# Long convolution by FFT, then a phase layer: group 0 takes h's spectrum from setup's tiles, and the e table is made during the first inverse

## Chip, cores and metric

One core of one Trainium2 chip. The metric is the device time of one execution in microseconds (us), the median of several runs. All inputs and outputs lie in the chip's memory in float32.

## What is computed

The input x has 8 batches of 5696 positions by 128 channels; h has 5696 positions by 128 channels. The reference, cut to what matters:

```python
L = 2 * S                                   # S = 5696
Yf = rfft(x, n=L, axis=1) * rfft(h, n=L, axis=0)[None]
x = irfft(Yf, n=L, axis=1)[:, :S, :]        # a causal convolution, channel by channel
theta = x @ w_theta
zr, zi = x * cos(theta), x * sin(theta)
y = einsum('ts,bsd->btd', w_tok_r, zr) + einsum('ts,bsd->btd', w_tok_i, zi)
u = x + y
out = u + maximum(u @ w_ch, 0)
```

The change touches only the convolution's front: the tables, the transform of h, and the first of eight groups.

## The kernel before

**Stages.** The transform of length 11392 is done as 178 by 64, by matrix products on TensorE (PE). The work is cut into eight groups: two batches (`bp`) times 64 of the 128 channels (`dh`). For each group: stage a (PE line L241: x times the table `f1_t`, sixteen chunks, evicted to the tile `a_` by ACT at L248 or by DVE at L246); stage b (L259, with the table `w_t2`, twelve chunks of eight frequencies: ACT copies a chunk to `xs` at L372, DVE multiplies it at L374 with the chunk `hs` of h's spectrum into the tiles `u_t` and `v_t`); stage c (L390 and L391, with the tables `r_u` and `r_v`, sixteen chunks, evicted to `g` by DVE at L398 or by ACT at L395 and L396, the latter ones alternately); stage d (L413, with the table `e_t`, evicted to `yt` by ACT at L416, and stored). Stage c needs every chunk of stage b. Beside stage c of one group runs stage a of the next, beside stage d its stage b. The loop over the groups is unrolled; `woven` lays several lists of steps into one order by their shares of an interval. All stages rotate four PSUM buffers of two banks.

**h.** h goes through stages a and b first (`h16`, then `h_chunk`, L297 and L299). `h_chunk` writes its twelve chunks into `u_t` and `v_t`, which the groups' products need later, and stores each with two DMAs into `hf_hbm` (L304). Every group then loads its half of a chunk from `hf_hbm` with two DMAs into one of four `hs` buffers (L365): four chunks ahead, and the chunk c+4 when chunk c has been multiplied. All these DMAs are issued by SP, in order.

**Tables.** `w_t2` comes in three blocks of fifteen frequencies: `w_angles(b)` takes four DVE operations (the third of them `below_one`, L164, and the rounding before it `up`, L161), `w_sines(b)` two on ACT, and `w_rest(b)` four copies or negations on DVE (L204 to L207). `e_t` (33 rows) comes in three steps of eleven rows: `e_index` on POOL (an index, a scaling, the rounding), `e_angles` on DVE, `e_table` as two sines on ACT (L170, L173); all three steps are woven into group 0's stage b. They use the pool `s2`.

**x.** `load_x` loads x for two batches by 16 DMAs that POOL issues (L133). There is one buffer `x16`, so the load for the next pair of batches waits until PE has read the old one, which is at the end of the odd group's stage a.

**Order.** Up to the end of group 0's stage a (`in_order`), DVE, ACT and POOL run in the order of the source. After that a scheduler orders each engine's instructions by priority. Within an engine everything starts in order, and an instruction that waits holds up all behind it. POOL executes its arithmetic and issues its DMAs from one queue.

Of the kernel before, what the change touches and what calls it, by code (L numbers as in the profile page):

```python
# [23 lines left out]
def kernel(  # L24
# [80 lines left out]
    def pool(name, bufs, stack, **kw):  # L105
        return stack.enter_context(tc.tile_pool(name=name, bufs=bufs, **kw))
# [5 lines left out]
    keep = pool("keep", 1, ctx, side="right")  # L112
    fc = pool("fft_c", 1, conv, side="right")
    fs = pool("fft_s", 2, conv, side="right")
    s1 = pool("set_1", 1, setup, side="right")
    s2 = pool("set_2", 3, setup, side="right")

    u_t = fc.tile([P, UVW + P], F16)
    v_t = fc.tile([P, UVW + P], F16)
# [31 lines left out]
    def pair_of(n, m=P):
        t = s2.tile([P, 11 * NB], F32, tag="turn", name="turn")[:m, :n]
        k = s2.tile([P, 11 * NB], F32, tag="whole", name="whole")[:m, :n]
        return t, k
# [5 lines left out]
    def up(t, k, eng=nc.vector):  # L160
        eng.tensor_scalar(k, t, MAGIC, None, op0=add)  # L161
# [15 lines left out]
    f1_t = fc.tile([P, 2 * K1], F16)  # L177
    odd = lane[:, 4:5]
    WS = 15
    w_of = [pair_of(WS * 32) for _ in range(KH // WS)]  # L180
    f_t, f_k = (z[:NB, :K1] for z in (s1.tile([P, K1], F32, name="f_t"), s1.tile([P, K1], F32, name="f_k")))
    o_t, o_k = s1.tile([P, 1], F32, name="o_t"), s1.tile([P, 1], F32, name="o_k")

    def slot(e, k1):
        return (k1 + e * KH) % K1

    def w_angles(b):
        t, k = w_of[b]
        nc.vector.tensor_scalar(t, k, lane[:, 2:3], lane[:, 3:4], op0=add, op1=mult)
        up(t, k)  # L190
        below_one(t, k)
        absolute(k, t)

# [13 lines left out]
            nc.vector.tensor_copy(w_t2[p0:p0 + 64, KH + s0:KH + s0 + WS],  # L207
                                  w_t2[64 - p0:P - p0, s0:s0 + WS])

    index(w_of[0][1], [[1, WS], [N1, 32]], 0)  # L210
    nc.vector.tensor_scalar(lane[:, 3:4], lane[:, 0:1], 1.0 / NF, None, op0=mult)
    w_angles(0)
    w_sines(0)
    index(f_k, [[1, K1]], 0)
    nc.vector.tensor_scalar(f_t, f_k, lane[:NB, 1:2], 1.0 / N1, op0=mult, op1=mult)
    up(f_t, f_k)
    below_one(f_t, f_k)
    absolute(f_k, f_t)
    sine(f1_t[:NB, K1:], f_t, -1)
    cosine(f1_t[:NB, :K1], f_k)  # L220
    for b in range(1, len(w_of)):
        index(w_of[b][1], [[1, WS], [N1, 32]], WS * b)
        w_angles(b)
        w_sines(b)
# [64 lines left out]
    nc.gpsimd.memset(hst[(NCK - 1) // 6][:, (NCK - 1) % 6], 0.0)  # L289

    def h_chunk(c):
        c0, ck = CHK[c]
        ps = f2(a_h, c, False)
        h_ = hst[c // 6][:, c % 6]
        dst = h_[:, :, :, :ck]
        if c % 3 == 1:
            nc.vector.tensor_scalar(dst, ps, 16.0 / NF, None, op0=mult)  # L297
        else:
            nc.scalar.activation(dst, ps, AF.Copy, scale=16.0 / NF)  # L299
        for cc, j in ((0, 0), (NCK - 1, CHK[-1][1] - 1)):  # L300
            if c == cc:
                nc.vector.tensor_scalar(dst[:, :, :, j], dst[:, :, :, j], 0.5, None, op0=mult)
        for ri in range(2):
            nc.sync.dma_start(  # L304
                hf_hbm[:, c, :, ri, :].rearrange("h p n -> p h n"),
                h_[64 * ri:64 * ri + 64].rearrange("p h d k -> p h (d k)"))

    for c in range(NCK):
        h_chunk(c)
    nc.gpsimd.memset(u_t[:, UVW:], 0.0)  # L310
    nc.gpsimd.memset(v_t[:, UVW:], 0.0)
# [4 lines left out]
    sgn = fc.tile([P, N2], F32)  # L316

    def r_table(n_, r_):
        t, k = pair_of(2 * N2)
# [12 lines left out]
    e_of = {}  # L332

    def e_index(n0):
        e_of[n0] = t, k = pair_of(11 * NB, K1)
        index(k, [[1, 11], [N2, NB]], n0)
# [8 lines left out]
    def e_table(n0):
        t3, k3 = (z.rearrange("p (n m) -> p n m", m=NB) for z in e_of[n0])
        sine(e_t[:K1, n0:n0 + 11, 1, :], t3, -1)
        cosine(e_t[:K1, n0:n0 + 11, 0, :], k3)
# [4 lines left out]

    LEAD = 4

    def stage_b(a_st, dh):

        hs_of = {}

        def load(c):  # L360
            if c >= NCK:
                return
            hs = hs_of[c] = fh.tile([P, 2, HD * CK], F16, tag="hs", name="hs")
            for e in range(2):
                nc.sync.dma_start(hs[64 * e:64 * e + 64], hf_hbm[dh, c])  # L365

        def chunk(c):
            c0, ck = CHK[c]
            hv = hs_of[c].rearrange("p r (d k) -> p r d k", k=CK)
            ps = f2(a_st, c)  # L370
            xs = fs.tile([P, 2, HD, CK], F16, tag="xs", name="xs")
            nc.scalar.activation(xs[:, :, :, :ck], ps, AF.Copy)  # L372
            for r in range(2):
                nc.vector.tensor_tensor(  # L374
                    uv[r][:, :, :, c0:c0 + ck], xs[:, :, :, :ck],
                    hv[:, r:r + 1, :, :ck].to_broadcast([P, 2, HD, ck]), op=mult)
            load(c + LEAD)
        return [lambda c=c: load(c) for c in range(LEAD)], [lambda c=c: chunk(c) for c in range(NCK)]
# [73 lines left out]

# [777 lines left out]
```

## Time and profile before

| | us |
|---|---|
| median of 3 runs (2083.46 to 2084.41) | 2083.66 |
| profiled execution | 2080.49 |
| its span, first to last instruction | 2078.7 |
| first PE instruction | 19.4 |
| h's stage b on PE, from | 34.1 |
| group 0: last product of stage b ends | 79.8 |
| group 0: stage c from, stage d from | 79.5, 100.9 |
| group 1: stage c from | 125.5 |

In the whole span PE is busy for 1960.0 us (94%), DVE for 1572.9 (76%), POOL for 921.9 (44%), ACT for 651.4 (31%). The granted clock of PE averages 0.983.

How to read it: the profile is of one execution. A line of the timeline has the start, the duration, the engine, the line of the kernel, the operation, the tiles written and read, the shape, how many instructions are merged in it, and in brackets how long the engine stood idle before it and what ended that. `SPq` and `POOLq` are instructions that only issue a DMA. Engines: PE is TensorE (PEld its weight loads), DVE is VectorE, ACT is ScalarE, POOL is GpSimd, SP is SyncE. The granted clock is the share of TensorE's full clock.

### The profile page before, as it was taken

How to read it: one execution, taken by the hardware profiler on the slowest of the kernel's cores; microseconds unless marked ns; L12 is line 12 of the kernel's file. 1: busy time of each engine (PE TensorE's matmuls, PEld its weight loads, DVE VectorE, ACT ScalarE, POOL GpSimd, SP SyncE). 2: the span in 40 equal slices, each digit the busy share in tenths (PEclk: the TensorE clock that was granted, in tenths of full speed). 3: DMA queues.
4: the chain of work that ended last, by engine and by line, in shares of the span. 5: the costliest groups of instructions: out<-in, count | busy, mean ns of one | idle time of the engine just before them, and what ended most of it. 6: DMA issues, size and time to landing. Idle time of an engine off the chain costs nothing.

```text
span 2078.7 us, 41648 instructions
## 1 busy us (share of the span) xinstructions
PE 1960.0 (94%) x15853; PEld 1079.2 (52%) x15853; DVE 1572.9 (76%) x2874; ACT 651.4 (31%) x989; POOL 921.9 (44%) x1663
## 2 busy tenths in 40 slices
PE   4688988889999999999999999899999999999998
PEld 4677888754444444444444444344444444444444
DVE  8666767777788888888877666877868677777767
ACT  5677878873333333333310000011111111111111
POOL 7302011257445454545466654445453535445450
PEclk9899999999999999999999999999999999999999
DMA  9879595989899999999999899778696978878793
GB/s 128 140 127 176 137 144 175 245 260 238 144 179 167 183 168 170 169 182 169 181 164 161 127 210 256 125 124 154 126 156 127 153 130 148 145 138 150 129 156 88
DMA packets 454312, 334.98 MB, mean 161 GB/s; under 512 B 134823, under 2 KB 407335, under 8 KB 453127
## 3 DMA queue, kind: packets, MB, share of 16 engines
q0 software_dynamic: 272032, 156.73, 57.2%
q1 hardware_dynamic: 176096, 164.05, 27.5%
q10 hardware_dynamic: 5984, 11.54, 1.6%
q8 instruction: 124, 2.03, 0.4%
q14 instruction: 76, 0.62, 0.1%
HBM read 377.11 MB, written 92.49 MB: 226 GB/s over the span
## 4 chain that ended last, share of the span: by engine, by line
PE 68%; DMA 3%; DVE 3%; POOL 2%; issue 2%; ACT 0%; DVEq 0%; ACTq 0%; SPq 0%; POOLq 0%
PE m L1167 61%; PE m L1088 2%; DMA b<-z_hbm 1%; DMA ring<-in_moe_w_tok_r_dram 1%; DVE c L1174 1%; DVE b L723 1%; PE v L869 1%; PE utp L862 1%; PE m L1171 1%; POOL ring L577 1%; POOL b L513 1%; DVE wt L782 1%; PE theta_ps L464 0%; PE tpz L810 0%; POOL y_hbm L651 0%
## 5 line engine op out<-in xcount | busy, mean ns | idle before, releaser
L577 POOL DMA_DIRECT2D ring<-in_moe_w_tok_i_dram x720 | 388.7, 546 | 655.6 <-DVE wt L782 571.7
L577 POOL DMA_DIRECT2D ring<-in_moe_w_tok_r_dram x720 | 387.2, 545 | 141.8 <-DVE wt L782 77.8
L782 DVE STREAM_TRANSPOSE wt<-ring 128x384 f32<-128x384 f32 (+2 forms) x720 | 359.3, 523 | 117.3 <-PE m L1167 68.2
L1167 PE MATMUL m<-b,wt 128*128 128x512 bf16 x1640 | 389.7, 380 | 2.0 <-DVE wt L782 1.7
L1167 PEld LDWEIGHTS <-wt 128*128 128x128 bf16 x1804 | 176.4, 98 | 219.8 <-DVE wt L782 7.8
L1174 DVE TENSOR_TENSOR c<-c,m 128x512 f32<-128x512 f32 x412 | 265.0, 668 | 0.4 <-PE m L1167 0.4
L864 ACT ACTIVATE ring<-utp 128x512 bf16<-128x512 bf16 x85 | 50.8, 597 | 581.9 <-PE utp L862 581.9
L390 PE MATMUL ps<-r_u,u_t 128*128 128x128 f16 x1024 | 122.4, 220 | 9.0 <-ACT red L487 3.7
L133 POOL DMA_DIRECT2D x<-in_x_dram x64 | 51.8, 818 | 166.4 <-PE ps L241 152.5
L391 PE MATMUL ps<-r_v,v_t 128*128 128x128 f16 x1024 | 121.4, 220 | 0.4
L1088 PE MATMUL m<-b,wt 128*128 128x512 bf16 x480 | 113.7, 387 | 7.5 <-DMA b<-z_hbm 4.4
L859 ACT ACTIVATE ub<-c 128x512 bf16<-128x512 f32 x88 | 55.1, 628 | 191.8 <-DMA ring<-in_moe_w_tok_r_dram 113.1
L391 PEld LDWEIGHTS <-v_t 128*128 128x128 f16 x1024 | 100.3, 98 | 9.6 <-issue 8.0
L390 PEld LDWEIGHTS <-u_t 128*128 128x128 f16 x1024 | 100.5, 98 | 4.2 <-DVE u_t L374 2.4
L374 DVE TENSOR_TENSOR u_t<-xs,hs 128x1024 f16<-128x1024 f16 x96 | 64.2, 668 | 50.4 <-DMA hs<-hf_hbm 25.6
L372 ACT ACTIVATE xs<-ps 128x1024 f16<-128x1024 f32 x96 | 91.4, 977 | 27.1 <-DVE v_t L374 12.3
L1088 PEld LDWEIGHTS <-wt 128*128 128x128 bf16 x528 | 51.5, 100 | 68.8 <-issue 11.0
L259 PEld LDWEIGHTS <-w_t 64*128 64x128 f16 x3240 | 60.7, 102 | 37.9 <-issue 31.6
L466 ACT ACTIVATE red<-theta_ps,magic 128x512 f32<-128x512 f32 (+1 forms) x46 | 31.6, 687 | 134.4 <-PE theta_ps L464 106.4
L812 ACT ACTIVATE ring<-tpz 128x512 bf16<-128x512 bf16 (+1 forms) x46 | 27.5, 597 | 131.1 <-PE tpz L810 110.6
L374 DVE TENSOR_TENSOR v_t<-xs,hs 128x1024 f16<-128x1024 f16 x96 | 63.6, 662 | 4.0 <-DMA hf_hbm<-v_t 4.0
L488 ACT ACTIVATE mag<-mag,half_pi 128x512 f32<-128x512 f32 (+1 forms) x90 | 65.6, 729 | 0.0
(2913 smaller groups left out, 3803.9 us busy)
## 6 DMA issues: line engine op xcount, KB each, us to landing
ring<-in_moe_w_tok_r_dram POOLq DMA_DIRECT2D x352, 96.0 KB, 4.5
ring<-in_moe_w_tok_i_dram POOLq DMA_DIRECT2D x352, 96.0 KB, 4.9
ring<-in_moe_w_tok_r_dram POOLq DMA_DIRECT2D x352, 80.0 KB, 4.4
ring<-in_moe_w_tok_i_dram POOLq DMA_DIRECT2D x352, 80.0 KB, 3.8
hs<-hf_hbm SPq DMA_DIRECT2D x192, 128.0 KB, 3.2
cp_hbm<-c SPq DMA_DIRECT2D x88, 256.0 KB, 2.4
c<-cp_hbm SPq DMA_DIRECT2D x88, 256.0 KB, 4.3
out_dram<-c SPq DMA_DIRECT2D x88, 256.0 KB, 4.1
```

Source lines behind the costliest of these rows:

```text
L259: nc.tensor.matmul(ps[:, e, j * HD:(j + 1) * HD], w_t2[rows, slot(e, c0 + j), N2 * (1 - ri):N2 * (3 - ri)], a_st["a"][rows, ri * K1 + c0 + ...
L372: nc.scalar.activation(xs[:, :, :, :ck], ps, AF.Copy)
L374: nc.vector.tensor_tensor(uv[r][:, :, :, c0:c0 + ck], xs[:, :, :, :ck], hv[:, r:r + 1, :, :ck].to_broadcast([P, 2, HD, ck]), op=mult)
L390: nc.tensor.matmul(o, u_t[:, at:at + P], r_u, start=True, stop=False)
L391: nc.tensor.matmul(o, v_t[:, at:at + P], r_v, start=False, stop=True)
L488: nc.scalar.activation(mag, mag, AF.Sin, bias=half_pi[:m], scale=-TWO_PI)
L577: nc.gpsimd.dma_start(wb[32 * i:32 * i + 32, :ng, :nj * 64], bass.AP(tensor=a.tensor, offset=a.offset + row0 * S + p * H + i * QR + j0 * 6 ...
L782: nc.vector.transpose(wt.rearrange("p j t r -> p (j t r)").bitcast(F32).rearrange("p (j g t) -> p g j t", j=TJ, g=4)[:, :ng, :nj], wb[:, : ...
L859: nc.scalar.activation(ub[:m].rearrange("p b d -> p (b d)"), c[:m], AF.Copy)
L1088: nc.tensor.matmul(ms[n // 2 * 2 + h], a[n][:, j, :, r], bts_of[p][jj][n % 2 * 2 + h][:, r, :], start=(n % 2 == 0 and jj == 0 and r == 0), ...
L1167: nc.tensor.matmul(ms[q], a[q][:, j, :, r], bts[jj][q][:, r, :], start=(jj == 0 and r == 0), stop=(jj == NJ - 1 and r == 1 and q not in left))
L1174: nc.vector.tensor_tensor(c, z, ms[q], op=op)
```

## The change

1. h's spectrum stays in setup's tiles: chunks 0 to 7 in `h16`, 8 to 11 in the space of the w table's angles (`w_all`, which takes the place of the pool `s2`). It no longer passes through `u_t` and `v_t`.
2. Group 0 copies its half from there into `hs`, by four DMAs a chunk on SP (partition halves times real and imaginary part). The stores to `hf_hbm`, for the later groups, stand on SP between and behind the first four chunks' copies.
3. The e table is made in seven steps of five rows (the last has three), in the buffer of `yt`, now in a pool of its own. Step 0 stands in group 0's stage a, the other six in its stage c; through the first loop round DVE and ACT keep the order of the source.
4. The w table: one of its roundings moves from DVE to ACT (`w_turns`), the blocks are interleaved, `w_rest(2)` stands behind h's stage a, and DVE takes other chunks of the evictions. The 12 matmuls that keep PE busy at the end of stage b (L265) are left out for group 0.

The diff, cut to its core:

```diff
@@ the w table
-    w_of = [pair_of(WS * 32) for _ in range(KH // WS)]
+    WQ = WS * 32
+    w_all = s1.tile([P, 2 * KH // WS * WQ], F32, name="w_all")
+    w_of = [tuple(w_all[:, (2 * b + n) * WQ:(2 * b + n + 1) * WQ] for n in range(2)) for b in range(KH // WS)]
...
+    def w_turns(b):
+        t, k = w_of[b]
+        nc.vector.tensor_scalar(t, k, lane[:, 2:3], lane[:, 3:4], op0=add, op1=mult)
+        nc.scalar.activation(k, t, AF.Identity, bias=magic)
+
     def w_angles(b):
         t, k = w_of[b]
-        nc.vector.tensor_scalar(t, k, lane[:, 2:3], lane[:, 3:4], op0=add, op1=mult)
-        up(t, k)
         below_one(t, k)
         absolute(k, t)
...
@@ h
-    steps, a_h = stage_a(lambda q: h16[:NB].rearrange("p h n d -> p (h n) d")[:, :, q], (3, 6, 9, 12, 15))
+    steps, a_h = stage_a(lambda q: h16[:NB].rearrange("p h n d -> p (h n) d")[:, :, q], (4, 6, 8, 10, 12, 14))
     w_rest(1)
-    for n, f in enumerate(steps):
+    for f in steps:
         f()
-        if n == 3:
-            w_rest(2)
+    w_rest(2)
-    hst = [t[:, :6 * D * CK].rearrange("p (c h d k) -> p c h d k", c=6, h=2, k=CK) for t in (u_t, v_t)]
+    h_own, h_rest = h16.rearrange("p h n d -> p (h n d)"), w_all.bitcast(F16)
+    HC = D * CK
+    hst = [(h_own[:, c * HC:(c + 1) * HC] if c < 8 else h_rest[:, (c - 8) * HC:(c - 7) * HC]).rearrange(
+        "p (h d k) -> p h d k", h=2, k=CK) for c in range(NCK)]
...
-        if c % 3 == 1:
+        if c in (3, 5, 7, 9, 11):
...
@@ the e table
+    e_all = fy.tile([P, NB, N2], BF16, tag="yt", name="e_all").rearrange("p m n -> p (m n)").bitcast(F32)
+    E_STEPS = [(n, n0, min(ES, EN - n0)) for n, n0 in enumerate(range(0, EN, ES))]
+    def e_pair(n, cn):
+        return [e_all[:K1, (2 * (n % 3) + q) * ES * NB:][:, :cn * NB] for q in range(2)]
...
@@ stage b
             for e in range(2):
-                nc.sync.dma_start(hs[64 * e:64 * e + 64], hf_hbm[dh, c])
+                if own:
+                    for ri in range(2):
+                        nc.sync.dma_start(hs[64 * e:64 * e + 64, ri],
+                                          hst[c][64 * ri:64 * ri + 64, dh].rearrange("p d k -> p (d k)"))
+                else:
+                    nc.sync.dma_start(hs[64 * e:64 * e + 64], hf_hbm[dh, c])
...
@@ group 0
-    a0, load0, b0 = front(0, (2, 5, 8, 11, 14))
-    woven(a0, load0)
+    a0, load0, b0 = front(0, (2, 4, 6, 8, 10, 12, 14))
+    for c in range(NCK):
+        h_chunk(c)
+        if c < LEAD:
+            load0[c]()
+        h_store(c)
+    for e_ in E_STEPS[:3]:
+        e_index(*e_)
+    for n, f in enumerate(a0):
+        f()
+        if n == 9:
+            e_table(*E_STEPS[0])
     in_order.close()
-    e_steps = range(0, EN, 11)
-    for n0 in e_steps:
-        e_index(n0)
-    woven(b0, ([lambda n0=n0: e_angles(n0) for n0 in e_steps], 0.0, 0.6),
-          ([lambda n0=n0: e_table(n0) for n0 in e_steps], 0.1, 0.9),
-          ([s_table, lambda: r_table(0, r_u), lambda: r_table(1, r_v)], 0.3, 1.0))
+    in_order.enter_context(tc.manual_schedule(engines={mybir.EngineType.DVE, mybir.EngineType.Activation}))
+    woven(b0, ([s_table, lambda: r_table(0, r_u), lambda: r_table(1, r_v)], 0.0, 0.6),
+          [lambda: e_index(*E_STEPS[3])])
+    e_left = [lambda f=f, n=n: f(*E_STEPS[n]) for f, n in (
+        (e_table, 1), (e_index, 4), (e_table, 2), (e_index, 5), (e_table, 3), (e_index, 6),
+        (e_table, 4), (e_table, 5), (e_table, 6))]
...
@@ the loop over the groups
-        woven((c_, 0.06 if a_ else 0.0, 1.0), (a_, 0.0, 0.35 if dh == 0 else 0.55), now, load_)
+        woven((c_, 0.06 if a_ else 0.0, 1.0), (a_, 0.0, 0.35 if dh == 0 else 0.55), now, load_, ([] if g else e_left, 0.0, 0.9))
+        if g == 0:
+            in_order.close()
```

More of the change, by code (lines that the diff above doesn't have):

```diff
@@ L114 @@
     fs = pool("fft_s", 2, conv, side="right")
+    fy = pool("fft_y", 1, conv, side="right")
     s1 = pool("set_1", 1, setup, side="right")
-    s2 = pool("set_2", 3, setup, side="right")
     u_t = fc.tile([P, UVW + P], F16)
@@ L149 @@
     nc.vector.memset(lane[64:P, 2:3], float(KH))
[L151 to L154, printed above, removed]
     def index(k, pattern, base):
@@ L208, in w_rest @@
                                   w_t2[64 - p0:P - p0, s0:s0 + WS])
-    index(w_of[0][1], [[1, WS], [N1, 32]], 0)
-    nc.vector.tensor_scalar(lane[:, 3:4], lane[:, 0:1], 1.0 / NF, None, op0=mult)
[L212 to L224, printed above, removed]
+    nc.scalar.activation(f1_t[:, :1], zero_b, AF.Sin, bias=zero_b)
+    for b in range(len(w_of)):
+        index(w_of[b][1], [[1, WS], [N1, 32]], WS * b)
+        if b == 0:
+            index(f_k, [[1, K1]], 0)
+    nc.vector.tensor_scalar(lane[:, 3:4], lane[:, 0:1], 1.0 / NF, None, op0=mult)
     nc.vector.tensor_scalar(o_t, lane[:, 1:2], 0.5, None, op0=mult)
@@ L229 @@
     nc.vector.tensor_scalar(odd, o_k, -4.0, 1.0, op0=mult, op1=add)
+    w_turns(0)
+    nc.vector.tensor_scalar(f_t, f_k, lane[:NB, 1:2], 1.0 / N1, op0=mult, op1=mult)
+    up(f_t, f_k)
+    below_one(f_t, f_k)
+    absolute(f_k, f_t)
+    w_turns(1)
+    w_angles(0)
+    w_sines(0)
+    sine(f1_t[:NB, K1:], f_t, -1)
+    cosine(f1_t[:NB, :K1], f_k)
+    w_turns(2)
+    w_angles(1)
+    w_sines(1)
+    w_angles(2)
+    w_sines(2)
     w_rest(0)
@@ L280 @@
                               u_t[:NB, :N2 * D].rearrange("p (n h d) -> p h n d", h=2, d=HD)[:, :, :, d0:d0 + 32])
-    steps, a_h = stage_a(lambda q: h16[:NB].rearrange("p h n d -> p (h n) d")[:, :, q], (3, 6, 9, 12, 15))
+    steps, a_h = stage_a(lambda q: h16[:NB].rearrange("p h n d -> p (h n) d")[:, :, q], (4, 6, 8, 10, 12, 14))
     w_rest(1)
-    for n, f in enumerate(steps):
+    for f in steps:
         f()
-        if n == 3:
-            w_rest(2)
-    hst = [t[:, :6 * D * CK].rearrange("p (c h d k) -> p c h d k", c=6, h=2, k=CK) for t in (u_t, v_t)]
-    nc.gpsimd.memset(hst[(NCK - 1) // 6][:, (NCK - 1) % 6], 0.0)
+    w_rest(2)
[3 more added lines that the diff above has]
+        "p (h d k) -> p h d k", h=2, k=CK) for c in range(NCK)]
+    nc.gpsimd.memset(hst[NCK - 1], 0.0)
+    nc.gpsimd.memset(u_t[:, UVW:], 0.0)
+    nc.gpsimd.memset(v_t[:, UVW:], 0.0)
     def h_chunk(c):
@@ L293, in h_chunk @@
         ps = f2(a_h, c, False)
-        h_ = hst[c // 6][:, c % 6]
+        h_ = hst[c]
         dst = h_[:, :, :, :ck]
-        if c % 3 == 1:
+        if c in (3, 5, 7, 9, 11):
             nc.vector.tensor_scalar(dst, ps, 16.0 / NF, None, op0=mult)
@@ L302, in h_chunk, with h_store @@
                 nc.vector.tensor_scalar(dst[:, :, :, j], dst[:, :, :, j], 0.5, None, op0=mult)
+    def h_store(c):
         for ri in range(2):
@@ L305, in h_chunk @@
                 hf_hbm[:, c, :, ri, :].rearrange("h p n -> p h n"),
[L306 to L311, printed above, removed]
+                hst[c][64 * ri:64 * ri + 64].rearrange("p h d k -> p h (d k)"))
     r_u = fc.tile([P, P], F16)
@@ L318, in r_table @@
     def r_table(n_, r_):
-        t, k = pair_of(2 * N2)
+        t, k = (s1.tile([P, 2 * N2], F32, name=f"r_{n_}{q}") for q in "tk")
         index(k, [[0, 2], [1, N2]], 0)
@@ L330, in r_table, with e_index, e_table @@
         nc.vector.tensor_scalar(r_[:, N2 + EN:], k[:, N2 + EN:], -0.125, None, op0=mult)
[L332 to L336, printed above, removed]
+    ES = 5
+    e_all = fy.tile([P, NB, N2], BF16, tag="yt", name="e_all").rearrange("p m n -> p (m n)").bitcast(F32)
+    E_STEPS = [(n, n0, min(ES, EN - n0)) for n, n0 in enumerate(range(0, EN, ES))]
+    def e_pair(n, cn):
+        return [e_all[:K1, (2 * (n % 3) + q) * ES * NB:][:, :cn * NB] for q in range(2)]
+    def e_index(n, n0, cn):
+        t, k = e_pair(n, cn)
+        index(k, [[1, cn], [N2, NB]], n0)
         nc.gpsimd.tensor_scalar(t, k, lane[:K1, 1:2], 1.0 / NF, op0=mult, op1=mult)
         up(t, k, nc.gpsimd)
-    def e_angles(n0):
-        t, k = e_of[n0]
+    def e_table(n, n0, cn):
+        t, k = e_pair(n, cn)
         below_one(t, k)
         absolute(k, t)
[L345 to L348, printed above, removed]
+        t3, k3 = (z.rearrange("p (n m) -> p n m", m=NB) for z in (t, k))
+        sine(e_t[:K1, n0:n0 + cn, 1, :], t3, -1)
+        cosine(e_t[:K1, n0:n0 + cn, 0, :], k3)
     def s_table():
@@ L354, with stage_b @@
     LEAD = 4
-    def stage_b(a_st, dh):
+    def stage_b(a_st, dh, own=False, warm=True):
         hs_of = {}
@@ L369, in chunk @@
             hv = hs_of[c].rearrange("p r (d k) -> p r d k", k=CK)
-            ps = f2(a_st, c)
+            ps = f2(a_st, c, warm)
             xs = fs.tile([P, 2, HD, CK], F16, tag="xs", name="xs")
@@ L403, in chunk @@
             if n0 == 0:
-                st["yt"] = fg.tile([P, NB, N2], BF16, tag="yt", name="yt")
+                st["yt"] = fy.tile([P, NB, N2], BF16, tag="yt", name="yt")
             g_, yt = st["g"], st["yt"]
@@ L438, in front @@
         steps, a_st = stage_a(lambda q: x16[:NB, :, dh * HD + q], on_dve)
-        return (steps, *stage_b(a_st, dh))
-    a0, load0, b0 = front(0, (2, 5, 8, 11, 14))
-    woven(a0, load0)
-    in_order.close()
-    e_steps = range(0, EN, 11)
-    for n0 in e_steps:
-        e_index(n0)
-    woven(b0, ([lambda n0=n0: e_angles(n0) for n0 in e_steps], 0.0, 0.6),
-          ([lambda n0=n0: e_table(n0) for n0 in e_steps], 0.1, 0.9),
-          ([s_table, lambda: r_table(0, r_u), lambda: r_table(1, r_v)], 0.3, 1.0))
+        return (steps, *stage_b(a_st, dh, g == 0, g > 0))
+    a0, load0, b0 = front(0, (2, 4, 6, 8, 10, 12, 14))
[10 more added lines that the diff above has]
+            e_table(*E_STEPS[0])
+    in_order.close()
+    in_order.enter_context(tc.manual_schedule(engines={mybir.EngineType.DVE, mybir.EngineType.Activation}))
[4 more added lines that the diff above has]
+        (e_table, 4), (e_table, 5), (e_table, 6))]
     setup.close()
```

## The prediction

> **What bounds the kernel now.** I read the page first: PE busy 94% of the span, but section 2 shows its first slices (52 us each) at 4 to 8 tenths, and the edits all lie before the second group's inverse. The rest of the span keeps its instruction order in the changed kernel, so what the front gains or loses is carried to the end. Then the timeline of the first 130 us, SP's own timeline, POOL's, and the stretches table. All times are us from the span's start in the profiled execution.
>
> The timeline round group 0's product with h's spectrum:
>
> ```profile
> 59.13 0.69 DVE L374 TENSOR_TENSOR u_t<-xs,hs 128x1024 f16<-128x1024 f16 x1 [4.85 <-DMA hs<-hf_hbm]
> ...
> 63.82 0.69 DVE L374 TENSOR_TENSOR v_t<-xs,hs 128x1024 f16<-128x1024 f16 x1 [4.00 <-DMA hf_hbm<-v_t]
> ...
> 65.70 1.03 PE L259 MATMUL ps<-a__702,w_t 64*128 64x64 f16 x32 [9.79 <-ACT xs L372]
> ...
> 79.36 0.41 DVE L374 TENSOR_TENSOR v_t<-xs,hs 128x256 f16<-128x256 f16 x1
> ```
>
> DVE waits for the reload of h's spectrum, then for its last copy to leave v_t; PE stands 9.79 us. Group 0's products end at 79.77, and its inverse can start only then. SP, which issues these transfers:
>
> ```profile
> 37.40 9.21 SPq L304 DMA_DIRECT2D hf_hbm<-u_t  x12
> 46.71 7.41 SPq L304 DMA_DIRECT2D hf_hbm<-v_t  x10
> 54.17 6.37 SPq L365 DMA_DIRECT2D hs<-hf_hbm  x8
> 60.63 1.28 SPq L304 DMA_DIRECT2D hf_hbm<-v_t  x2
> ```
>
> These 32 issues took 24.27 us, 0.76 each with short waits in it; the last two, back to back, 0.64 each. The source view gives the issue itself (min/median/max, ns): first for these loads (32 issues of 54 to 84 us), their landing, and then for a copy from one on-chip tile to another later in the kernel:
>
> ```profile
> L365 SPq DMA_DIRECT2D hs<-hf_hbm x32: 444/595/1893, 54.2 to 81.2; - x32
> DMA to landing us min/median/max: 2.5/2.8/4.1
> ```
>
> ```profile
> L513 SPq DMA_DIRECT2D b<-zz x31: 600/600/1170, 441.6 to 485.8; - x31
> ```
>
> The price is per issue, 0.60 with some 0.05 between two, and source and size don't change it. That makes SP a queue to count.
>
> After the products, the inverse of group 0 (stage c, with group 1's stage a beside it), then stage d with group 1's stage b:
>
> ```profile
> 79.50:88.60 9.10, 8.18 (x112) 7.54 (x113) 5.04 (x5) 7.99 (x13) 0.00 (x0) 1.00 0.29 88
> 88.60:100.90 12.30, 11.45 (x224) 11.23 (x224) 9.51 (x9) 6.70 (x11) 9.88 (x13) 1.00 1.45 128
> 100.90:124.80 23.90, 17.56 (x471) 15.58 (x472) 14.02 (x22) 15.61 (x19) 2.25 (x4) 0.79 1.35 158
> 145.80:161.20 15.40, 14.17 (x470) 12.40 (x471) 12.18 (x20) 14.20 (x17) 0.00 (x0) 1.00 0.44 126
> ```
>
> (length, then busy PE, PEld, DVE, ACT, POOL, granted clock, DMA share, GB/s.) The third and fourth rows are the same work, one group apart: 23.9 with the next x in flight and the clock at 0.79, 15.4 without. POOL issues that x when group 1's stage a has read the old one:
>
> ```profile
> 88.72 7.63 POOL L133 DMA_DIRECT2D x<-in_x_dram  x10 [16.88 <-PE ps L241]
> ...
> 102.84 1.50 POOL L133 DMA_DIRECT2D x<-in_x_dram  x2 [1.20 <-DMA x<-in_x_dram]
> ```
>
> 16 issues from 88.72 to 104.34: 15.6 us in which POOL does nothing else.
>
> **Part 1, setup and h's forward transform.** DVE's chain to w_rest(0)'s end at 17.72 loses three L161 (start to start 0.83 + 0.56 + 0.71 = 2.1; ACT, idle there, takes them) and puts the five one-column operations (1.0) partly into the wait for the first index (0.62 idle before L189); a wait for ACT's third addition costs some 0.5. Net 2.2: w_rest(0) ends at 15.5, h16's copy (2.71) at 18.3, PE starts near 17.1 instead of 19.35. Then h's stage a, in DVE's timeline:
>
> ```profile
> 25.11 0.83 DVE L204 TENSOR_SCALAR w_t<-w_t,lane 128x960 f16<-128x960 f16 x1
> ...
> 27.24 3.44 DVE L207 COPY w_t<-w_t 64x2880 f16<-64x2880 f16 x2
> 30.71 3.35 DVE L246 CAST a__184<-ps 128x720 f16<-128x720 f32 x4
> ```
>
> Before, w_rest(2) (25.11 to 30.68) stands between DVE's evictions, and they end at 34.06. After: w_rest(1) 3.9 (20.39 to 24.26) to 22.2, six evictions at 0.84 to 27.2, then w_rest(2): 3.9 by the row of w_rest(1), 5.6 by its own, which ran beside POOL's arithmetic; POOL computes then too, so 5.0, to 32.2. The halving of chunk 0's first column, behind it on DVE, costs 0.47 to 1.12 by L302; I take 0.5. So chunk 0 of h's spectrum is ready at 32.7 (31.6 to 33.9), where SP's first store began at 37.40. Group 0's stage a would end near 45 instead of 50.9, and its 24 products at 0.62, with r's and sgn's rows about 17, near 62. This is what the change could bring, if the spectrum came in time.
>
> **Part 2, SP.** Reads from h's own tiles take four issues a chunk (two halves of partitions times real and imaginary), not two. In SP's order in the changed kernel: 16 loads for chunks 0 to 3 with 8 stores between them, then the other 16 stores, and only then 32 loads for chunks 4 to 11. 72 issues stand up to the last load, where 48 stood. No compute holds them: the chunks come at about 1 us and SP needs 3 to 4 for each, and a load of chunk c+4 needs chunk c's products, done by then. At 0.65 (floor) 46.8, at 0.76 (the four rows) 54.7; I take 0.72, since part of 0.76 was waiting: 51.8. Last issue ends at 84.5; landing 2.6 after its start at 83.8 is 86.5; the two small products (0.42 and 0.38) and their semaphore 0.9: 87.4, against 79.77: **7.6 later**. Ends: 31.6 + 46.8 + 2.7 = 81.1 (1.4 later) and 33.9 + 54.7 + 3.8 = 92.4 (12.6 later). The stall on v_t is gone; all of part 1's gain lies under SP.
>
> A rule speaks against this edit: the Trainium skill, page "DMA: Bandwidth & Descriptors", section "Rules for kernel authors", says not to split a transfer into two partition halves, since both use the same DMA engines anyhow, and to coalesce small ones. The trace agrees in so far as an issue costs 0.60 whatever it moves; with two issues a chunk the sum would be 56 issues, 40.3, and the products would end near 76, earlier than before.
>
> **Part 3, the e table in stage c.** Six steps of the table (five rows wide, 445 elements; the last 267) move behind the products, in a hand-written order on DVE and ACT. ACT pays two sines a step: 1.10 for 979 wide and 0.70 for 480 give 0.65 each for 445. Two steps lie ahead of the end of group 1's stage a: 2.6, and 0.8 for DVE's part of the first; less 1.4, two evictions done while SP was awaited. PE starts stage c at half clock, since it stood idle before and the 12 warming matmuls (L265, 3.79) are dropped; up to 1.7 more. The x load, POOL's next work, also stands behind e_index(5), which waits for the second step. Before it started 8.95 after the products' end; I take 13.
>
> The costly part is the last step. Its e_index is placed on POOL behind the 16 x issues: 13 + 15.6 + some 2.0 (by POOL's 0.63, 1.09, 2.67 rows, scaled) = 30.6 after the products' end. Its DVE operations stand ahead of DVE's last two evictions of stage c, its sines ahead of ACT's last one. Stage c would otherwise be done near 24. Then 0.8 on DVE, two evictions at 1.2 and a semaphore: stage d starts 34 after the products' end, where it was 21.2 (100.93 - 79.77): **12.8 later**. What follows gets cheaper, since the x transfers have nearly drained: 15.4 by the undisturbed row, 2.5 for a clock that fell in the 10 us wait, 0.6 for late spectra = 18.5 instead of 23.8: **5.3 back**. Net 7.5; ends 2 (x starts 10.5 after, 16 for the stage) and 11.
>
> The Trainium skill, page "TensorE: Matmul & The Clock Gate", section "What's actually happening", gives about 3.4 us of sustained activity to full clock; by it each cold start costs 1.7. The table of stretches shows 0.79 over 23.9, which is 10 us at half clock and up to 5 lost; both ends stand in the range.
>
> **Sum.** 7.6 + 7.5 = 15.1 slower. The profiled execution took 2080.49 (span 2078.7, 1.8 round it): 2095.6 by its own account. The median shown is 2083.66, 3.2 above it: **2098.8**. A difference under 0.2% (4.2 us) can't be told from none.
>
> **Rivals.** (a) The last table step costs nothing net: the wait is repaid in full because stage d and group 1's products no longer meet the x transfers. For it: 8.5 us between the two rows above. Against: PE stands 10 us meanwhile and comes back cold. 7.6 + 1 gives 2092; 0.20. (b) The other side: SP isn't the bound, because a short on-chip copy issues faster than the trace's rows. Then the products end near 63 by DVE, 17 earlier, and with part 3's 7.5 the sum is 9.3 faster, 2074. It needs a pitch under 0.38 ((63 - 3 - 32.7) / 72); above 0.62 there is no gain left on SP at all ((79.8 - 2.7 - 32.7) / 72). For: the fastest rows, 0.44. Against: L513's on-chip copies at 600 in minimum and median; 0.07. (c) In between, within 0.2%: a pitch near 0.55 with part 3 as forecast; 0.05. (d) SP at its upper end and cold clocks on top: 2107 or more; 0.08. That leaves 0.60 for the forecast.
>
> **Numbers.** Faster 0.07, same 0.05, slower 0.88. The range 2088 to 2106 leaves out (b), (c) and (d); both unknown prices, 1.4 to 12.6 and 2 to 11, seldom meet at one end.
>
> **What would show it.** Right: SP issuing without a break from about 33 to 84; DVE's products of chunks 4 to 11 spaced by about 2.9 and waiting for DMA hs; half clock there; then ACT or DVE waiting some 7 us for POOL's e_all near the end of stage c; the next group's stage b free of waits for hs. Wrong: products ending before 79.8, or no wait on e_all. h's forward transform should end 4 to 6 earlier in any case.

## Result and the profile after

The changed kernel took 2098.91 us in the median (2094.38 to 2099.95, 4 runs), the kernel before, beside it, 2084.03 (2083.46 to 2084.95): a ratio of 1.0067, 95% interval 1.0055 to 1.008. A second set of runs gave 1.0053 (1.0041 to 1.0066). The change makes the kernel slower by 11 to 15 us; 2098.8 was forecast.

The profiled execution took 2094.38 (span 2092.6), against 2080.49 (span 2078.7): 13.9 more. First SP's timeline of the changed kernel (start, length, queue, line, operation, tiles, number of issues; L377 are the loads from setup's tiles, L316 the stores, L380 the loads from `hf_hbm`, L389 the products):

```profile
30.72 3.34 SPq L377 DMA_DIRECT2D hs<-h  x4
34.10 1.30 SPq L316 DMA_DIRECT2D hf_hbm<-h  x2
...
47.99 7.90 SPq L316 DMA_DIRECT2D hf_hbm<-h  x10
55.99 5.22 SPq L316 DMA_DIRECT2D hf_hbm<-w_all  x8
61.31 10.15 SPq L377 DMA_DIRECT2D hs<-h  x16
71.56 10.99 SPq L377 DMA_DIRECT2D hs<-w_all  x16
```

SP issues without a break from 30.72 to 82.55: 72 issues in 51.8. What that does to DVE's products, and how long the on-chip copies take from issue to landing (source view of L377):

```profile
64.70 0.69 DVE L389 TENSOR_TENSOR u_t<-xs,hs 128x1024 f16<-128x1024 f16 x1 [11.75 <-DMA hs<-h]
...
67.23 0.69 DVE L389 TENSOR_TENSOR u_t<-xs,hs 128x1024 f16<-128x1024 f16 x1 [1.24 <-DMA hs<-h]
...
84.05 0.41 DVE L389 TENSOR_TENSOR v_t<-xs,hs 128x256 f16<-128x256 f16 x1 [0.21 <-DMA hs<-w_all]
```

```profile
DMA to landing us min/median/max: 2.0/2.0/3.5
```

Chunk 4's product waits 11.75, while SP issues the rest of eighteen stores in a row and then that chunk's loads. Chunks 4 to 11 follow at a mean spacing of 2.7, and the last product ends at 84.45. Then the stretches (start:end, length, then busy PE, PEld, DVE, ACT, POOL, granted clock, DMA share, GB/s): the first part of stage c, the wait at its end, and stage d with group 1's products.

```profile
83.90:93.50 9.60, 8.29 (x67) 8.08 (x68) 3.76 (x5) 6.72 (x10) 2.54 (x3) 0.50 0.40 109
...
110.20:120.60 10.40, 0.65 (x33) 0.55 (x33) 4.28 (x6) 3.87 (x7) 4.82 (x7) 0.68 1.94 169
120.60:139.40 18.80, 16.70 (x481) 14.70 (x481) 13.05 (x22) 16.27 (x21) 0.00 (x0) 0.90 0.50 128
```

PE works through the first 9.6 us of stage c at half clock, and it does 0.65 us of work in the 10.4 before stage d. POOL and DVE there:

```profile
99.78 7.69 POOL L133 DMA_DIRECT2D x<-in_x_dram  x10
...
113.84 1.50 POOL L133 DMA_DIRECT2D x<-in_x_dram  x2 [1.72 <-DMA x<-in_x_dram]
115.35 0.42 POOL L152 IOTA e_all<- 90x267 f32 x1
```

```profile
117.39 0.43 DVE L159 SCALAR_TENSOR_TENSOR e_all<-e_all 90x267 f32<-90x267 f32 x1 [3.18 <-POOL e_all L156]
```

The last step's index follows the sixteenth x issue directly, and DVE stands for it, with the last two evictions of stage c behind it.

The difference adds up at the start of group 1's stage c (139.4; before 125.5, so 13.9). Stage c starts 4.4 later (83.9, was 79.5). From there to stage d it is 36.7 (was 21.4), 15.3 more. From stage d to group 1's stage c it is 18.8 (was 24.6), 5.8 less.

### The profile page after: what moved, and what is told of

Same layout as the page of the kernel before. It is cut to its first block, busy times and chain, and to the rows that moved or that the text cites. A ratio compares the mean times of both kernels' runs of the same rounds, so it can differ in the third digit from the quotient of the medians.

```text
span 2092.6 us, 41514 instructions
## 1 busy us (share of the span) xinstructions
PE 1950.9 (93%) x15664; PEld 1084.0 (52%) x15841; DVE 1572.7 (75%) x2883; ACT 652.5 (31%) x997; POOL 920.1 (44%) x1675
## 4 chain that ended last, share of the span: by engine, by line
PE 63%; DVE 4%; DMA 3%; issue 2%; POOL 1%; ACT 0%; DVEq 0%
PE m L1194 59%; DMA ring<-in_moe_w_tok_r_dram 2%; DVE c L1201 1%; DVE b L750 1%; PE utp L889 1%; PE v L896 1%; PE m L1198 1%; POOL ring L602 1%; DVE wt L809 1%; PE theta_ps L489 0%; PE tpz L837 0%; PE m L1081 0%; PE m L1115 0%; DMA zl<-zl_hbm 0%; DMA wl<-in_moe_w_tok_i_dram 0%
## 5 line engine op out<-in xcount | busy, mean ns | idle before, releaser
L809 DVE STREAM_TRANSPOSE wt<-ring 128x384 f32<-128x384 f32 (+2 forms) x720 | 359.4, 524 | 111.9 <-PE m L1194 67.4
L1194 PE MATMUL m<-b,wt 128*128 128x512 bf16 x1599 | 385.9, 380 | 4.2 <-DVE wt L809 1.7
L891 ACT ACTIVATE ring<-utp 128x512 bf16<-128x512 bf16 x85 | 50.7, 597 | 582.2 <-PE utp L889 582.2
L1115 PE MATMUL m<-b,wt 128*128 128x512 bf16 x466 | 110.2, 382 | 11.0 <-DVE wt L809 3.6
L886 ACT ACTIVATE ub<-c 128x512 bf16<-128x512 f32 x88 | 55.1, 628 | 192.9 <-DVE c L1156 114.2
L389 DVE TENSOR_TENSOR u_t<-xs,hs 128x1024 f16<-128x1024 f16 x96 | 64.1, 668 | 63.5 <-ACT xs L387 26.8
L265 PEld LDWEIGHTS <-w_t 64*128 64x128 f16 x3240 | 60.9, 102 | 39.3 <-issue 33.2
L247 PE MATMUL ps<-f_t,x 89*128 89x180 f16 x512 | 55.6, 254 | 11.9 <-ACT xs L387 8.3
```

Of the source, the lines that this page charges most:

```text
L247: nc.tensor.matmul(ps[:, i // 2, (i % 2) * 2 * K1:(i % 2 + 1) * 2 * K1], lhs(q + i), f1_t[:NB], start=True, stop=True)
L265: nc.tensor.matmul(ps[:, e, j * HD:(j + 1) * HD], w_t2[rows, slot(e, c0 + j), N2 * (1 - ri):N2 * (3 - ri)], a_st["a"][rows, ri * K1 + c0 + ...
L389: nc.vector.tensor_tensor(uv[r][:, :, :, c0:c0 + ck], xs[:, :, :, :ck], hv[:, r:r + 1, :, :ck].to_broadcast([P, 2, HD, ck]), op=mult)
L809: nc.vector.transpose(wt.rearrange("p j t r -> p (j t r)").bitcast(F32).rearrange("p (j g t) -> p g j t", j=TJ, g=4)[:, :ng, :nj], wb[:, : ...
L1115: nc.tensor.matmul(ms[n // 2 * 2 + h], a[n][:, j, :, r], bts_of[p][jj][n % 2 * 2 + h][:, r, :], start=(n % 2 == 0 and jj == 0 and r == 0), ...
L1194: nc.tensor.matmul(ms[q], a[q][:, j, :, r], bts[jj][q][:, r, :], start=(jj == 0 and r == 0), stop=(jj == NJ - 1 and r == 1 and q not in left))
```

## Experiments

Each kernel is the changed one with the edit shown. Places in single executions are from the profiles. What follows group 1's stage c took 1951.7 to 1959.6 in the fourteen profiles (1953.2 before and after, 1951.7 in a second execution of the changed kernel). The four kernels with e5's order of x have 1955.3 to 1957.2 there; whether that comes from the edit, single executions don't tell. So a part of the front is judged in its own stretch, which the two executions of the changed kernel repeat within 0.6, and a whole kernel by its ratio. "c to c" is the time from group 0's stage c to group 1's.

| | last product ends | stage c | x issued | stage d | group 1's stage c | c to c | ratio to before (95%) |
|---|---|---|---|---|---|---|---|
| before | 79.8 | 79.5 | 88.7–104.3 | 100.9 | 125.5 | 46.0 | |
| changed | 84.5 | 83.9 | 99.8–115.3 | 120.6 | 139.4 | 55.5 | 1.0067 (1.0055–1.008) |
| e0_after | 84.7 | 84.1 | 100.1–115.9 | 121.1 | 140.0 | 55.9 | 1.0053 (1.0041–1.0066) |
| e1_pool_stores | 72.8 | 72.2 | 88.3–102.8 | 108.1 | 127.0 | 54.8 | 1.0019 (1.0007–1.003) |
| e2_hbm_first | 71.3 | 71.0 | 85.5–102.3 | 107.6 | 126.7 | 55.7 | 1.0008 (0.9997–1.002) |
| e3_last_early | 84.4 | 83.8 | 95.4–110.5 | 116.8 | 136.2 | 52.4 | 1.005 (1.0033–1.0067) |
| e4_e_in_b | 89.2 | 91.2 | 101.4–117.3 | 113.7 | 136.5 | 45.3 | 1.006 (1.0045–1.0075) |
| e5_x_late | 83.7 | 83.1 | 97.4–115.8 | 112.0 | 138.2 | 55.1 | 1.0056 (1.0043–1.0069) |
| e6_warm | 85.2 | 85.1 | 97.6–111.9 | 117.2 | 135.8 | 50.7 | 1.0051 (1.0039–1.0063) |
| e7_mix | 66.7 | 66.5 | 79.4–97.0 | 93.3 | 117.5 | 51.0 | 0.9951 (0.9938–0.9964) |
| e8_no_e | 86.8 | 86.3 | 97.7–113.5 | 110.0 | 134.3 | 48.0 | 1.004 (1.0027–1.0053) |
| e9_late_warm | 84.0 | 83.5 | 96.0–114.2 | 110.6 | 137.1 | 53.6 | 1.0082 (1.0065–1.0098) |
| e10_mix_cold | 66.8 | 66.5 | 81.4–98.6 | 95.3 | 119.0 | 52.5 | 0.998 (0.9967–0.9994) |
| e11_no_x | 85.5 | 84.9 | none | 112.3 | 130.9 | 46.0 | 1.0033 (1.0014–1.0052) |

e0_after is the changed kernel again: 

> The changed kernel itself, as the measure for the other three on the same chip. 13 to 16 us above the kernel before (1.0065 to 1.0075); group 0's products end near 84, stage d near 120, the second group's stage c near 139.

The places came as expected. The time did not: 10.6 above the kernel before, and the ratio, 1.0053, lies under the expected range. So whole times of two sets differ by some 4 us in this comparison.

### SP's issues

e1_pool_stores: the 24 stores are issued by POOL, behind the first three index steps.

```diff
-            nc.sync.dma_start(
+            nc.gpsimd.dma_start(
                 hf_hbm[:, c, :, ri, :].rearrange("h p n -> p h n"),
...
-        h_store(c)
     for e_ in E_STEPS[:3]:
         e_index(*e_)
+    for c in range(NCK):
+        h_store(c)
```

> The changed kernel, but h's 24 stores to hf_hbm are issued by POOL behind its first three e_index steps; SP keeps only the 48 copies from h's own tiles. Theory 1 (the number of issues on SP times 0.72 sets the end of group 0's products): 30.7 + 48 x 0.72 + 2 of landing + 0.5 = 68 instead of 84.5, the rest as in the changed kernel, so 16 faster than it, near 2078 to 2080 in the profile. Theory 2 (the on-chip copies' own transfer, or DVE and ACT in stage b, sets it): the products still end at 80 or later and the time moves by less than 4.

e2_hbm_first: the stores first, then all of group 0's loads from `hf_hbm`, two a chunk.

```diff
-        return (steps, *stage_b(a_st, dh, g == 0, g > 0))
+        return (steps, *stage_b(a_st, dh, False, g > 0))
...
         h_chunk(c)
-        if c < LEAD:
-            load0[c]()
         h_store(c)
+    for f in load0:
+        f()
```

> The changed kernel, but group 0 loads its half of h's spectrum from hf_hbm like the other groups, two loads a chunk behind all 24 stores; the spectrum still stands in setup's tiles, not in u_t and v_t. Theory 1: again 48 issues on SP, so the products end at 68 to 69, as in the run with POOL's stores (within 2): nothing comes from the on-chip source itself, only from u_t and v_t being free, and its four issues a chunk cost it all. Theory 2 (the way over HBM costs its round trip and the wait for the stores' landing): 3 or more later than the run with POOL's stores, over 71.

The last product ends 11.7 and 13.2 earlier than in the changed kernel. SP in e1, then in e2:

```profile
30.74 29.12 SPq L377 DMA_DIRECT2D hs<-h  x32
59.97 10.88 SPq L377 DMA_DIRECT2D hs<-w_all  x16
```

```profile
43.16 5.19 SPq L316 DMA_DIRECT2D hf_hbm<-w_all  x6
48.40 5.77 SPq L380 DMA_DIRECT2D hs<-hf_hbm  x8
54.28 1.28 SPq L316 DMA_DIRECT2D hf_hbm<-w_all  x2
```

The 48 own loads alone took 40.1 instead of the 34 to 35 that 0.72 each makes. After sixteen of them all four `hs` buffers are in use, and the next load waits for chunk 0's product: this wait of 3.3 was overlooked, and the products ended at 72.8, where 68 was expected. In e2 no load comes from the chip at all, and the products end earlier still, at 71.3, though not at the 68 to 69 of theory 1. So the 72 issues held the products, and the on-chip source by itself brought nothing. 24 issues less are worth 11.7 to 13.2 and not 17.3 (24 times 0.72), since SP then waits for products in places. Against the kernel before, which also has 48 issues, e2 is 8.5 ahead: its SP starts 6.6 earlier (30.8, was 37.4), and the wait of 4.0 for the stores out of `v_t` is gone. In both runs c to c stays near 55: the e table's cost is separate. By the whole time e1 gained 7 to 11 on the changed kernel, where theory 1 had 16.

### The wait for POOL

e3_last_early: the last e step has a tile of its own; its index stands in setup, its table in stage b.

```diff
...
-    for e_ in E_STEPS[:3]:
+    for e_ in E_STEPS[:3] + E_STEPS[6:]:
...
+          ([lambda: e_table(*E_STEPS[6])], 0.6, 0.6))
...
```

> The changed kernel, but the last e step (3 rows) has a tile of its own in setup's pool, its e_index stands on POOL with the first three, and its e_table in group 0's stage b, so that nothing in stage c waits for POOL behind the x loads. Products' end as in the changed kernel, 84.5. Theory 1 (the wait for e_all behind x is what costs): stage d starts 4 to 8 earlier than 120.6, and stage d with stage b of group 1 takes 3 to 5 longer than 18.8 because it meets x again: 1 to 4 faster in all. Rival (a) of the prediction (the wait is repaid in full): stage d earlier, but group 1's stage c starts at 139 to 140 as before and the time stays within 1.

The wait did not go; it changed its owner. With step 6 away, step 5's index stands behind the x issues, which begin 4.4 earlier:

```profile
113.33 0.62 DVE L159 SCALAR_TENSOR_TENSOR e_all<-e_all 90x445 f32<-90x445 f32 x1 [3.87 <-POOL e_all L156]
```

Stage d starts 3.8 to 4.3 earlier, and what follows takes 19.3, hardly longer than in the changed kernel (18.7 to 18.9); c to c is 52.4, 3.1 to 3.5 less. So e3 met neither expectation in full and could not decide: the wait is still there, and x goes out earlier as well. e5_x_late moves the x load instead.

```diff
-            a_ = a_ + [next_x]
+            if g:
+                a_ = a_ + [next_x]
+            else:
+                now = [next_x]
-        woven(..., now, load_, ([] if g else e_left, 0.0, 0.9))
+        woven(..., (now, 0.0 if g else 0.8, 1.0), load_, ([] if g else e_left, 0.0, 0.9))
```

> The changed kernel, but the load of the next x is emitted behind the last step of the e table, so that this step's index stands on POOL behind two x issues and not behind sixteen. Theory 1 (the wait for POOL's e_all is a loss that is repaid in part): the waits of DVE and ACT on e_all near the end of stage c go; stage d starts near 112 where the changed kernel has 120.6; it then meets the x transfers, so that it takes 22 to 24.6 to the second group's stage c (18.8 in the changed kernel): that stage starts 2 to 5 earlier, ratio to the changed kernel 0.9975 to 0.999. Rival (the prediction's rival a: the wait is repaid in full): stage d starts as early, but takes 27 to the next stage c, and the ratio to the changed kernel is 0.9995 to 1.0005.

Only four of the x issues are left ahead of the last index's end, DVE and ACT no longer wait for POOL there, and stage d starts at 112.0. Then comes this stretch:

```profile
112.00:138.20 26.20, 20.56 (x481) 18.33 (x481) 13.37 (x22) 16.61 (x20) 3.03 (x5) 0.70 1.07 160
```

26.2 where the changed kernel takes 18.8: of the 7.8 to 8.1 won ahead of stage d (28.9 from stage c instead of 36.7 to 37.0), 7.3 to 7.4 are given back. The ratio is that of the changed kernel. The rival held: the wait is repaid, nearly in full.

e11_no_x asks by what. It leaves out the next x's load.

```diff
-                x16s[bp + 1] = load_x(bp + 1)
+                x16s[bp + 1] = load_x(bp + 1) if g else x16s[0]
```

> The changed kernel without the load of the next x in group 0's stage c (groups 2 and 3 read the first x again); all else as it stands, so that neither the last e step waits behind x issues nor does any x transfer meet stage d and group 1's products. With the x load behind the last step, stage d started at 112.0 but took 26.2 to the second group's stage c, which came at 138.2. Theory X (the early start is repaid because the x transfers hold up the loads of h's spectrum and the stage): stage d starts at 110 to 113 and takes 15.5 to 18, the second group's stage c starts at 127 to 130 and h's loads there land within 3.5. Rival (it is repaid by something else that an early stage d meets, a cold PE or ACT's last table sines): 22 to 26 for stage d with group 1's products, the second group's stage c at 134 to 138.

Stage d starts at the same place, and the stretch is:

```profile
112.30:130.90 18.60, 16.39 (x480) 14.45 (x480) 14.39 (x24) 17.99 (x23) 0.00 (x0) 0.91 0.44 130
```

18.6, a little over the bound of theory X and far below the rival's. Loads of h's spectrum from issue to landing, for those issued from 100 to 140, e5 and then e11:

```profile
DMA to landing us min/median/max: 2.4/5.5/9.4
```

```profile
DMA to landing us min/median/max: 2.5/3.0/9.4
```

So it is the x load that repays the wait: with it, the spectrum's loads take longer and so does the stage. An early stage d only meets it sooner. How the 7.6 come about is not fully split. DVE's direct waits for the spectrum are 4.1 in e5 and 0.9 in e11; the granted clock, 0.70 against 0.91, stands in the rest, and PE is busy 4.2 longer for the same matmuls. The 46.0 from stage c to stage c in e11 is no sign that the table is free: the kernel before pays for its x load within its own 46.0.

### The e table's work and PE's clock

e4_e_in_b weaves steps 1 to 6 into group 0's stage b.

```diff
-          [lambda: e_index(*E_STEPS[3])])
+          [lambda: e_index(*E_STEPS[3])], (e_left, 0.35, 1.0))
...
-    ([] if g else e_left, 0.0, 0.9)
+    ([], 0.0, 0.9)
```

> The changed kernel, but steps 1 to 6 of the e table are woven into group 0's stage b, where DVE and ACT stand idle for SP, instead of its stage c. Products' end near 84.5. Theory 1 (the e table in stage c makes that stage longer): stage c takes 20 to 22 instead of 26.3, x starts 9 to 11 behind the products instead of 15.3, stage d near 107; stage d and b beside x take 23 to 24 again; 6 to 8 faster in all. Theory 3 (PE's half clock at the start of stage c makes it longer, since PE stood for SP and the warming matmuls are gone): stage c keeps 24 to 26, and the gain is 0 to 3.

c to c falls to 45.3, under the kernel before. But the products end at 89.2, and stage c starts another 2.0 behind them, since ACT makes the last step's sines ahead of its evictions. From the last product to group 1's stage c it is 47.3 (before 45.7, changed 54.9). Stage c itself took 21.0, as theory 1 had it; the gain at group 1's stage c was 2.9 to 3.5 and not 6 to 8. The products came late because each step's sines stand ahead of ACT's next `xs`, and DVE waits for that copy:

```profile
85.09 0.69 DVE L389 TENSOR_TENSOR u_t<-xs,hs 128x1024 f16<-128x1024 f16 x1 [1.77 <-ACT xs L387]
```

SP issues the last of its own loads at 81.3, earlier than in the changed kernel (82.6), so it isn't the bound there. The table doesn't fit for free into this stage b either.

e6_warm: the changed kernel with 56 warming matmuls behind group 0's last f2.

```diff
...
-        return (steps, *stage_b(a_st, dh, g == 0, g > 0))
+        return (steps, *stage_b(a_st, dh, g == 0, WARM if g else 56))
```

> The changed kernel, but with 56 warming matmuls behind group 0's last f2 (none in the changed kernel): PE works from about 71.5 to 82.5, while the products wait for the spectrum. Theory 1 (stage c is longer than forecast because PE comes to it at half clock): the granted clock is full before 78 and at stage c's start; stage c takes 3 to 5 less, about 22 instead of 26.3; but the last e step still waits for POOL behind the x issues, whose start is also set by the second e steps, so stage d starts only 1 to 4 earlier: ratio to the changed kernel 0.998 to 0.9995. Rival (stage c is long because of the e table's work on DVE and ACT, not the clock): stage c 25 or more, ratio within 0.0005 of 1.

The first part of stage c, now at full clock:

```profile
85.10:94.70 9.60, 8.10 (x108) 7.48 (x108) 6.18 (x9) 9.46 (x15) 2.56 (x3) 1.00 0.35 105
```

In as long a stretch PE does 108 matmuls, where it did 67. Stage d starts 32.1 after stage c instead of 36.7 to 37.0, and c to c is 50.7: 4.8 to 5.2 less. In this stretch theory 1 holds (stage c's matmuls end after 23.1 instead of 26.3). The whole time does not show it: 1.0051 beside 1.0053 for the changed kernel in the same set, as the rival had it. The rest of that execution was 4.4 to 5.9 longer than in the changed kernel's two, and a gain of 4 us is near what the whole time can tell; whether later work gives it back stays open.

e8_no_e leaves out steps 1 to 6 of the table.

```diff
-    for e_ in E_STEPS[:3]:
+    nc.gpsimd.memset(e_t[:K1, ES:], 0.01)
+    for e_ in E_STEPS[:1]:
...
-          [lambda: e_index(*E_STEPS[3])])
...
+    e_left = []
```

> The changed kernel with steps 1 to 6 of the e table left out (index steps on POOL, DVE's and ACT's operations); the table's places for them hold a constant. From stage c's start to the second group's stage c the kernel before takes 46.0, the changed one 55.5 to 55.9, the one with warming matmuls 50.7, the one with the x load behind the last step 55.1. Theory A (of the 9.5 to 9.9, some 5 are PE's half clock at the start of stage c and some 5 the table's work on DVE and ACT in stage c; the wait for POOL is repaid): 50 to 52 here, since the clock is still cold. Theory B (all of it is the table's work, and the warming helped because it let ACT work ahead): 45 to 47. Products end at 84 to 85 either way.

48.0, between the two theories:

```profile
86.30:92.10 5.80, 5.80 (x49) 5.80 (x50) 2.04 (x3) 2.20 (x3) 0.00 (x0) 0.50 0.62 181
```

PE is cold here too, but without the table's operations between the evictions it is never idle, and the clock rises after 5.8 instead of 9.6. Without the table, then, the cold start costs 2.0 (48.0 against 46.0); with PE warm, the table costs 4.7 (50.7 against 46.0); together they cost 9.5 to 9.9, some 3 more than the sum. That each makes the other worse is the plain reading, and neither theory had it. Part of the 3 can be chance: in e5, whose stage c begins with the same work, the clock rose after 6.8, and in the changed kernel's two executions after 9.6 and 9.8 (see the clock rule below).

e9_late_warm is e5's and e6's edits together. 

> The changed kernel with both the 56 warming matmuls and the x load behind the last e step. Theory A (the wait for POOL's e_all has no net price): 50 to 51.5 from stage c's start to the second group's stage c, as with the warming alone (50.7), though stage d starts 5 to 9 earlier. Rival (the wait costs its price once PE is warm): 45 to 48.

Stage d starts 27.1 after stage c, the shortest of the kernels with the whole table but e4 and e7. But it takes 26.5 to group 1's stage c, against 18.6 in e6, so that c to c is 53.6, worse than with the warming alone. Neither expectation was met. It bears out e5: taking the wait away brought nothing, and here cost 2.9. The granted clock in that last stretch was 0.57, lower than e5's 0.70, while DVE waited for the spectrum for only 1.3.

### A version that beats both

e7_mix takes the findings together: own loads for chunks 0 to 3 only, two loads a chunk from `hf_hbm` after that, stores by POOL, e5's order of x, and 14 warming matmuls.

```diff
...
-                if own:
+                if own and c < LEAD:
...
-            nc.sync.dma_start(
+            nc.gpsimd.dma_start(
                 hf_hbm[:, c, :, ri, :].rearrange("h p n -> p h n"),
...
```

> All causes taken away at once: chunks 0 to 3 of group 0's half come from setup's tiles (16 loads on SP), chunks 4 to 11 from the copy in HBM (16 loads), the 24 stores are issued by POOL behind the first three index steps, the next x is emitted behind the last e step, and 14 warming matmuls stand behind group 0's last f2. Theory 1 (SP's 72 issues, the x issues ahead of the last e step and the cold clock make up the loss): SP issues 32 loads, products run on DVE from 46.5 nearly without a break and end at 64 to 67, stage d starts at 88 to 92, the second group's stage c at 112 to 117, 8 to 13 ahead of the kernel before (125.5): ratio to the kernel before 0.994 to 0.9965. Rival (what is won at the front is given back, because the x transfers then meet stage d and group 1's products, or POOL's own work is late): ratio to the kernel before 0.998 to 1.002, products at 70 or more or stage d with group 1's products 28 or more.

e10_mix_cold is the same without the 14. 

> The combination e7 without its 14 warming matmuls. Theory A (PE then comes to stage c at half clock, as in the changed kernel): half clock until 7 to 10 after stage c's start, 53 to 56 from stage c's start to the second group's stage c (51.0 with them), ratio to the kernel before 0.996 to 0.998 instead of 0.9951. Rival (PE is kept warm by the f2 matmuls of the close products, and the 14 do nothing): 50 to 52, ratio 0.9945 to 0.996.

e7 took 2074.2 against 2084.48 for the kernel before: 0.9951 (0.9938 to 0.9964), as theory 1 had it; stage d (93.3) and group 1's stage c (117.5) came just behind its bounds. Stage c and stage d with group 1's products, in e7 and then in e10:

```profile
66.50:93.30 26.80, 20.28 (x338) 19.24 (x338) 21.29 (x27) 21.80 (x36) 16.60 (x22) 0.98 0.63 79
93.30:117.50 24.20, 18.80 (x480) 16.74 (x481) 13.29 (x22) 16.32 (x20) 3.01 (x5) 0.74 1.13 170
```

```profile
66.50:95.30 28.80, 23.27 (x336) 22.15 (x337) 21.42 (x27) 21.45 (x36) 16.58 (x22) 0.86 0.60 75
```

The products end 13.1 earlier than in the kernel before, and 5.0 of that is lost in c to c. Without the warming, stage c to stage d is 2.0 longer and c to c 1.5 longer; the clock rises 7.6 after stage c's start, as theory A had it, while c to c, 52.5, lies between the two expectations. The two kernels ran beside different runs of the kernel before, so the ratios alone (0.9951 and 0.998) don't price the matmuls.

## Why the prediction was right or wrong

- **Which part bounds.** Right: all of the difference arises ahead of group 1's stage c, 13.9 there and 13.9 at the end. That the rest repeats so well in this pair is chance; over the profiles it spreads over 8.
- **Part 1.** Right, somewhat more was gained: PE starts at 16.0 (17.1 forecast), h's last eviction starts 6.9 earlier (36.7, was 43.6; 4 to 6 forecast). `w_rest(2)` took 3.5, not 5.0. So SP starts at 30.72, 2.0 ahead of the forecast. As forecast, none of it survives SP.
- **Part 2.** The count and the price were exact: 72 issues, 51.8. Oversized were the start (2.0) and the landing (1.0: the products end 1.9 after the last issue, not 2.9; an on-chip copy lands after 2.0, where 2.6 was taken, and one small product with its wait took 0.5, where two with 0.9 were taken). So 4.7 stands where 7.6 was forecast. e1 and e2 show the cause. The prediction's count for two loads a chunk was wrong: 24 stores and 24 loads are 48 issues and not 56; e2 has just these, and its products end at 71.3, not near 76. The Trainium skill, "DMA: Bandwidth & Descriptors", "Rules for kernel authors", says not to split a transfer into partition halves, because both use the same DMA engines. e2 bears out that fewer transfers help (its products end 13.2 earlier), but it still has one load for each half, and what it relieves is the issuing queue; that shared DMA engines cost anything here, no run shows.
- **Part 3, the sizes.** x starts 15.3 after the products' end (13 forecast), its issues take 15.6 and the index 2.0 as forecast, and stage d comes 36.2 after the products (34). The step that failed is "up to 1.7 more" for the cold clock. That figure came from no row of this case. Half clock lasted until 9.6 into stage c, and e6 prices it at about 5 with the table's work there, e8 at 2.0 without. Counted from the products' end, as in the prediction, stage d is 15.0 later where 12.8 was forecast, and 5.8 come back where 5.3 were: the net is 9.2 instead of 7.5. The 23.8 that the prediction took for the kernel before is short: its row ends at 124.8, and from stage d to group 1's stage c it is 24.6.
- **Part 3, the cause.** Wrong, though the net came out near. The costly part was said to be the wait for the last step. e5 takes that wait away and gains 0.4 to 0.8, and e11 shows why: the x transfers. Rival (a) described this mechanism and was given 0.20; its time, 2092, missed because it left nothing for what the changed kernel pays besides: the table's operations among the evictions, and the clock, 9.5 to 9.9 together from stage c to stage c.
- **The sum.** 15.1 against 13.9 by the profiles: one term 2.9 too large, the other 1.7 too small. That they nearly cancel is luck. The median of the runs agrees to 0.1, closer than the method allows.
- **The clock rule.** In the fourteen traces every stretch of half clock up to 140 is a whole multiple of 3.41 long; the 40.96 up to 93.5 in the changed kernel are twelve. So in these traces the clock rises only at the end of such a step. The last three of the twelve:

```profile
83.27:86.69 3.42, 2.49 (x20) 2.29 (x21) 1.99 (x5) 1.68 (x3) 0.38 (x1) 0.50 0.68 174
86.69:90.10 3.41, 2.41 (x20) 2.41 (x20) 0.95 (x1) 2.95 (x5) 2.16 (x3) 0.50 0.51 150
90.10:93.51 3.41, 3.41 (x30) 3.41 (x28) 1.22 (x1) 2.10 (x3) 0.00 (x0) 0.50 0.00 0
```

PE was busy for 2.49, 2.41 and 3.41, and the clock rose behind the one step without a gap. In e6 (matmuls from 72.19, full clock at 77.0) and e8 (stage c from 86.3, full clock at 92.1) it also rose at the end of the first step that PE filled. The Trainium skill, "TensorE: Matmul & The Clock Gate", "What's actually happening", gives about 3.4 us of sustained activity to full clock. The trace agrees: the 4.8 in e6, 5.8 in e8 and 9.6 in the changed kernel are the wait for one filled step of 3.41, and where the steps fall against stage c's start is chance. How full a step must be stays open: a step with PE busy for 3.17 did not raise the clock in e2 and e10, one with 2.99 did in e5.

Not settled: whether the 5 us that e7 still loses from stage c to stage c are DVE's and ACT's time or their order; no run tried another order.

## What to carry to other kernels

Count issues on a queue before counting bytes: four small on-chip copies in place of two loads cost the queue twice, and nothing comes back when the queue is the bound. Before pricing a wait, ask what the waiting work would meet if it came earlier; if that is a transfer which must drain anyway, the wait is nearly free. Work that is "hidden" in a stage of evictions still makes gaps in PE, and in the changed kernel the steps of 3.41 with such gaps kept the clock at half.

## What was unexpected of the hardware

The issues of SP took 0.72 in the mean over 72 in a row, with a median of 0.595 and single ones up to 1.77; the last eight stores from `w_all` took 0.65 each, the two rows of sixteen on-chip copies 0.63 and 0.69. On-chip copies landed 2.0 after their issue in minimum and median (3.5 at most), loads of h's spectrum from HBM after 2.4 or more. The granted clock stayed at half from 52.5 to 93.5 in the changed kernel although PE was busy for 86% of the last 9.6 of these 41 us: two steps of 3.41 with gaps passed before one without.
